# A two-stage Fourier filter and routed experts on one core: which of the first two batches keeps its data on chip between which stages, with one chain of stage 2 for both

## The chip, the core and the metric

The kernel runs on one core of a Trainium2 chip. The metric is the device time of one execution in microseconds (us). A core has four compute engines that run their own instruction queues in order and wait for each other by semaphores: TensorE (PE; its weight loads are listed as PEld), VectorE (DVE), ScalarE (ACT) and GpSimd (POOL). A fifth queue, SyncE (SP), only starts transfers (DMAs). ACT and POOL start transfers too; in the views such starts stand under SPq, ACTq or, for POOL's indirect ones, under POOL itself.

## What is computed

There are 8 batches of 2496 rows with 256 channels. Along the rows each batch is filtered in the frequency domain, and each filtered row then goes through a two-layer network that its token's number selects among 8:

```python
X = np.fft.rfft(x, axis=1)
Y = X * (filt_r + 1j * filt_i)[None]
y = np.fft.irfft(Y, n=2496, axis=1).reshape(8 * 2496, 256)
expert = token_ids * 2654435761 % 8
out[expert == e] = np.maximum(y[expert == e] @ w1[e], 0) @ w2[e]    # for e in 0..7, hidden size 1024
```

All data are float32.

## The kernel before, in words

**The Fourier part** is split into a length of 39 and a length of 64 (39 x 64 = 2496), by matrix products with tables, so each batch has three stages:

- *Stage 1* transforms along 39. Six steps (`u` = 0 to 5) take the batch's rows x, which `load1` brings in three pieces (`v` = 0, 1, 2) of up to 8 x 256 columns.
- *Stage 2* transforms along 64, multiplies by the filter and transforms back along 64. It has ten steps. `forward` (L253) makes two matmuls into pb and four DVE instructions: y = pb x filt (L264), two halves of z (L267), y = y + z (L268). `back` (L271) or `back_c` (L326) makes the matmuls into pc, which ACT copies out. Step u of `stage2` runs forward(u) and then back(u - 1), so that DVE works while PE goes on.
- *Stage 3* transforms back along 39 in six steps (`stage3`, L360): matmuls into pd, a copy into a tile o, the token's own number beside each row (L364), and then one scatter (an indirect DMA of POOL, L377) for each group of rows. It writes each row to its place in the DRAM table xs, where the rows are sorted by expert. A batch has 22 scatters.

Between the stages the axes change places: what lay on partitions must lie along the free axis. There are two ways to do this.

- *Through DRAM*: the stage writes its result to a DRAM tile (d1 after stage 1, d2 after stage 2; ACT starts these writes), and the next one reads it in another layout (`load2`, L245, into t2 tiles; `load4`, L355, into t4 tiles; SP starts these reads). Batches 2 to 7 take this way twice. Stage 1 is then `stage1` (L233) and stage 2's end is `back`.
- *On chip*: stage 1 is written with x as the stationary operand (`stage1_c`, L300), its result `mixed` stays in SBUF, and `turn2` (L316) transposes the columns for two steps of stage 2 on PE, with a copy by ACT. In the same way `back_c` leaves its result `out` in SBUF and `turn4` (L335) transposes it for stage 3. Batches 0 and 1 take this way twice.

**The order.** Nothing is scheduled automatically: a list `todo` (L669 to L694) holds each piece of work with a number, is sorted by it, and is issued in that order. Negative numbers come before the first tile of the expert part, numbers from 0 on are placed in the loop over tiles: `step(i)` issues what has a number below i + 1 between the two layers of tile i. Each engine then works its own queue in that order. Routing has its pieces in the list, too: `count` and `route` (DVE) find each token's expert and place, `later` (POOL, L551) sums corrections, `places` (L558) sends the places to DRAM and back as scatter indices sidx, `experts` finds each tile's expert.

```python
todo += [(-150.4, lambda: first.turn2(0)), (-130.5, lambda: second.turn2(0))]
todo += part2(0, spaced(-150, -130, N_2)) + part2(1, spaced(-130, -105, N_2))
todo += [(t, lambda u=u: second.stage1_c(u)) for u, t in enumerate(spaced(-147.5, -132, NU))]
for bt, at in ((first, spaced(-126, -105, NU)), (second, spaced(-103, -85, NU))):
    todo += [(t - 2.6, lambda bt=bt, u=u: bt.turn4(u)) for u, t in enumerate(at)]
    todo += [(t, lambda bt=bt, u=u: bt.stage3(u)) for u, t in enumerate(at)]
todo += part1(2, spaced(-102, -87, NU), [-128, -127, -126])
```

So batch 0's stage 2 runs first, batch 1's next with batch 0's stage 3 among it, then batch 1's stage 3 with batch 2's stage 1. After that `begin` (L703) starts the fetch of the first tiles' rows.

**The expert part.** Tile i holds 128 rows of one expert from xs. `load` fetches two tiles at once into xg (L729, four DMAs) and their row numbers (L731), `turn` transposes them on DVE into xt (L743), `up` (L753) makes 16 matmuls into ups, which ACT and DVE copy with the maximum against 0 (L757, L759), `down` (L765) makes the second layer, and POOL scatters the result to the output (L769). `weights` (L405, L407) loads an expert's two matrices, 1 MB each, two tiles ahead and only where the expert changes. Tiles 0 to 29 need the rows of batches 0 and 1 alone; a tile's fetch waits for the scatters of its batches. Batches 2 to 7 are worked on inside this loop.

**Buffers that matter.** The tiles `mid` and `wts` are shared by hand: `mixed`, `out`, t1, t2 and g tiles and x of batch 0 are slices of them, and the weights of the first two tiles later take `wts`. The o tiles of batches 0 and 1 have four buffers. The semaphores of transfers go round: the SP and ACT queues have eight together, and a DMA waits for the eighth before it, so no more than eight of theirs are under way; POOL's have eight of their own.

Of the kernel before, what the change touches and what calls it, by code (L numbers as in the profile page):

```python
# [19 lines left out]
P = 128  # L20
# [95 lines left out]
def kernel(  # L116
# [20 lines left out]
    def pool(stack, name, bufs, space=None):  # L137
# [33 lines left out]
             "g": [mid[:, k, :].rearrange("p (s c) -> p s c", c=C) for k in (9, 4)]}  # L171
# [5 lines left out]
    class Batch:  # L177


        def __init__(self, b):  # L180
            self.b = b
            self.d1 = self.d2 = None
            self.x, self.t2, self.t4, self.p = {}, {}, {}, {}
            self.g = None
            if b < 2:

                own = mid[:, 5 * b:5 * b + 5, :].rearrange("p k f -> p (k f)")
                self.mixed = own.rearrange("p (h n s) -> p h n s", h=2, s=NS)
                after = (held[:, 0:NS * C] if b == 0 else mid[:, 0:5, :].rearrange("p k f -> p (k f)"))
                self.out = after.rearrange("p (h n s) -> p h n s", h=2, s=NS)  # L190

        def load1(self, v):
# [9 lines left out]
            for h in range(H):  # L202
                nc.sync.dma_start(out=xt[h:NR:H, 0:n, :],
# [41 lines left out]
        def load2(self, g):  # L245
            t2 = slot("t2")
# [6 lines left out]
        def forward(self, u):  # L253
            ps = fps.tile([P, 2, C], F32, name=f"pb_{self.b}_{u}", tag="f")
            for i in range(2):
                s = 2 * u + i
                rhs = self.t2[u][:, i, :] if self.b < 2 else self.t2[s // SG][:, s % SG, :]
# [13 lines left out]
        def back(self, u):  # L271
# [4 lines left out]
            if u % half == 0:  # L276
                self.g = slot("g")
# [12 lines left out]
        def stage2(self, u):  # L290
            if self.b < 2 and u + 1 < NS // 2:
                self.turn2(u + 1)
            if u < NS // 2:
                self.forward(u)
            if u > 0:
                (self.back_c if self.b < 2 else self.back)(u - 1)
# [3 lines left out]
        def stage1_c(self, u):  # L300
# [4 lines left out]
            for h in range(2):  # L305
                ps = (xps, dps)[h].tile([P, 4, TB], F32, name=f"pa_{self.b}_{u}_{h}", tag="xd"[h])
# [28 lines left out]
        def turn4(self, u):  # L335
# [3 lines left out]
            copy = nc.vector.tensor_copy if self.b else nc.scalar.copy  # L339
            for k in range(0, min(XG, HN + 1 - XG * u), 2):  # L340
# [8 lines left out]
                if rows[0] == rows[1]:  # L349
                    copy(out=self.t4[v][:, j0 + k:j0 + k + 2, :], in_=ps[0:NK])  # L350
                else:
                    for i in range(2):
                        copy(out=self.t4[v][0:rows[i], j0 + k + i, :], in_=ps[0:rows[i], i, :])
# [30 lines left out]
    batches = [Batch(b) for b in range(B)]  # L384

# [28 lines left out]
    for v in range(NV):  # L414
        batches[0].load1(v)
# [4 lines left out]
    nc.scalar.dma_start(out=rt[:], in_=r_dram.ap())  # L420
    nc.vector.tensor_copy(tokno[:], rt[0:NR, G + 2 + NQP:])

    S_PARTS = (slice(0, 4), slice(4, 8), slice(8, 14), slice(14, NS))

    def load_tables(part):
        sl = S_PARTS[part]
# [4 lines left out]
    def load_filter(k, sl):  # L431
        filt = (filt_r, filt_i)[k]
        for q in range(2):
            off, step = (0, C) if q == 0 else (N1 * C, -C)
            nc.sync.dma_start(
# [200 lines left out]

    def part1(b, at, loads=None):
        bt = batches[b]
        if loads is None:
            loads = [at[2 * v] - 2.5 * (at[1] - at[0]) for v in range(NV)]  # L640
# [3 lines left out]
    def part2(b, at, ready=None):  # L644
# [5 lines left out]
        if b < 2:  # L650
# [188 lines left out]
```

## Time and profile before

| What | us |
|---|---|
| three timed runs | 1554.77 (median), 1554.59, 1556.4 |
| the profiled run, and the span of its profile | 1548.5, 1546.7 |
| PE busy, of the span | 1464.9 (95%) |
| DVE, ACT, POOL busy | 532.7 (34%), 234.0 (15%), 378.3 (24%) |
| first matmul of a tile starts | 165.34 |
| one tile in the last third of the loop | 7.03 |

The profile describes one execution. Its page gives busy times of each engine and the span in 40 slices; its views list instructions in order of time. A row of a timeline has start, duration, engine, line of the code, operation, output<-input, the number of instructions that it merges, and in brackets how long the engine stood idle before it and what ended that. The times of such a row are us from the span's start. "issue" in the brackets says that the profile shows nothing that was waited for. A PE row of a float32 product counts two records for each matmul (x8 for four). Shares of busy time over the whole span say little here, as the 165 us before the first tile and the loop after it have different limits; so the stretches are read one by one.

### The profile page before, as it was taken

The page shows a single profiled execution, that of the slowest core. Times are in us where ns is not written, and L with a number is a line of the kernel's source. Part 1 is how long each engine was busy: PE and PEld are TensorE (multiplying, and loading weights), DVE is VectorE, ACT ScalarE, POOL GpSimd, SP SyncE. Part 2 cuts the span into 40 slices and gives each one's busy share as a digit, 9 for nine tenths or more (in the row PEclk, how much of TensorE's full clock was granted, in tenths as well). Part 3 has the DMA queues.
Part 4 walks back from the last instruction along what each step waited for, and adds up shares of the span by engine and source line. Part 5 has one row for each costly group of instructions (what it writes and reads, how often), then busy time and mean ns, then how long its engine had stood idle before and what let it go on. Part 6 is the DMA issues. An engine that isn't in the chain of part 4 may idle for free.

```text
span 1546.7 us, 25542 instructions
## 1 busy us (share of the span) xinstructions
PE 1464.9 (95%) x9340; PEld 1339.3 (87%) x9340; DVE 532.7 (34%) x1004; ACT 234.0 (15%) x401; POOL 378.3 (24%) x384
## 2 busy tenths in 40 slices
PE   7796898989989999999999999999999999999997
PEld 6785687878878999899989999899899999999996
DVE  6772532542244434334333433222212121212121
ACT  4453121112111111101110111000000000000000
POOL 5466102312320133122221323232211111111111
PEclk9998899999999999999999999999999999999999
DMA  8256567548866794684737845552426523132324
GB/s 219 56 182 196 163 198 217 154 131 237 236 197 185 224 277 122 180 226 127 219 90 205 249 117 157 113 160 80 147 75 216 150 55 115 50 96 84 101 84 136
DMA packets 226476, 240.72 MB, mean 156 GB/s; under 512 B 123788, under 2 KB 200127, under 8 KB 219229
## 3 DMA queue, kind: packets, MB, share of 16 engines
q1 hardware_dynamic: 186451, 164.06, 38.6%
q0 software_dynamic: 19120, 43.35, 8.3%
q10 hardware_dynamic: 20778, 31.64, 6.6%
q8 instruction: 76, 1.25, 0.4%
q14 instruction: 51, 0.42, 0.1%
HBM read 415.94 MB, written 75.08 MB: 317 GB/s over the span
## 4 chain that ended last, share of the span: by engine, by line
PE 83%; DMA 6%; issue 5%; DVE 4%; SPq 1%; POOL 0%; ACT 0%; ACTq 0%; DVEq 0%; POOLq 0%
PE ups L753 34%; PE dps L765 33%; PE pb L258 3%; PE pd L220 3%; PE pc L280 3%; PE pa L220 2%; DMA d<-mid 2%; DVE z L267 1%; PE pc L331 1%; DMA wts<-in_x_dram 1%; DMA wts<-in_moe_w_dram 1%; DVE y L268 1%; DMA mid<-d 1%; DVE y L264 1%; PE pa L310 1%
## 5 line engine op out<-in xcount | busy, mean ns | idle before, releaser
L753 PEld LDWEIGHTS ups<-xt,wts 128*128 128x128 f32 x5088 | 594.3, 192 | 14.3 <-issue 3.0
L753 PE MATMUL ups<-xt,wts 128*128 128x128 f32 x5088 | 595.5, 275 | 4.4 <-issue 2.3
L765 PE MATMUL dps<-wts,ht 128*128 128x256 f32 x2544 | 580.1, 381 | 0.6 <-DMA wts<-in_moe_w_dram 0.6
L765 PEld LDWEIGHTS dps<-wts,ht 128*128 128x128 f32 x2544 | 479.8, 191 | 65.8 <-issue 2.4
L769 POOL DMA_INDIRECT out_dram<-osb,no x159 | 156.2, 982 | 883.2 <-DVE osb L768 829.8
L759 DVE TENSOR_SCALAR ht<-ups 128x512 f32<-128x512 f32 x159 | 110.0, 692 | 527.5 <-PE ups L753 512.8
L757 ACT ACTIVATE ht<-ups 128x512 f32<-128x512 f32 x159 | 95.0, 597 | 981.1 <-PE ups L753 741.1
L377 POOL DMA_INDIRECT xs<-o,sidx x176 | 177.0, 1006 | 240.6 <-DVE o L222 148.1
L768 DVE COPY osb<-dps 128x256 f32<-128x256 f32 x159 | 67.5, 425 | 366.2 <-PE dps L765 337.0
L267 DVE TENSOR_TENSOR z<-pb,filt 64x512 f32<-64x512 f32 x160 | 110.2, 689 | 3.5 <-DMA xs<-blank,at_i 1.1
L258 PE MATMUL pb<-mid,d_t 128*128 128x256 f32 x240 | 65.5, 398 | 12.0 <-DMA mid<-d 6.9
L220 PE MATMUL pd<-t,wi_t 120*117 120x256 f32 x320 | 76.0, 380 | 0.4 <-issue 0.4
L264 DVE TENSOR_TENSOR y<-pb,filt 128x512 f32<-128x512 f32 x80 | 54.1, 676 | 62.9 <-PE pb L258 49.0
L280 PE MATMUL pc<-y,e_t 128*128 128x256 f32 x240 | 64.7, 393 | 9.8 <-DVE y L268 8.1
L743 DVE STREAM_TRANSPOSE xt<-xg 128x256 f32<-128x256 f32 x159 | 69.1, 435 | 0.0
L220 PEld LDWEIGHTS pd<-t,wi_t 120*117 120x117 f32 x320 | 55.8, 181 | 10.8 <-issue 1.1
L280 PEld LDWEIGHTS pc<-y,e_t 128*128 128x128 f32 x240 | 45.8, 195 | 20.0 <-issue 6.6
L258 PEld LDWEIGHTS pb<-mid,d_t 128*128 128x128 f32 x240 | 45.0, 199 | 19.3 <-issue 14.0
L283 ACT COPY mid<-pc 128x512 f32<-128x512 f32 x60 | 35.2, 586 | 169.7 <-PE pc L280 163.4
L268 DVE TENSOR_TENSOR y<-y,z 128x512 f32<-128x512 f32 x80 | 59.2, 740 | 2.7
L220 PE MATMUL pa<-x,wf_t 117*120 117x256 f32 x224 | 53.1, 380 | 2.7 <-DMA x<-in_x_dram 1.9
L220 PEld LDWEIGHTS pa<-x,wf_t 117*120 117x120 f32 x224 | 39.6, 183 | 10.0 <-issue 2.7
(117 smaller groups left out, 456.0 us busy)
## 6 DMA issues: line engine op xcount, KB each, us to landing
wts<-in_moe_w_dram SPq DMA_DIRECT2D x322, 1024.0 KB
xg<-xs SPq DMA_DIRECT2D x316, 64.0 KB
mid<-d SPq DMA_DIRECT2D x60, 256.0 KB
d<-mid ACTq DMA_DIRECT2D x60, 256.0 KB
d<-mid ACTq DMA_DIRECT2D x12, 960.0 KB
t<-d SPq DMA_DIRECT2D x12, 960.0 KB
x<-in_x_dram SPq DMA_DIRECT2D x36, 312.0 KB
x<-in_x_dram SPq DMA_DIRECT2D x21, 234.0 KB
```

What stands on the lines that cost most here:

```text
L220: nc.tensor.matmul(out=ps[0:cols * H, k, :], lhsT=w[:], rhs=src[:, 2 * i + k, :], start=True, stop=True)
L258: nc.tensor.matmul(out=ps[:, i, :], lhsT=d_t[:, s, :], rhs=rhs, start=True, stop=True)
L264: nc.vector.tensor_tensor(out=y[:], in0=ps[:], in1=f_t[0][:, sl, :], op=OP.mult)
L267: nc.vector.tensor_tensor(out=z[b], in0=ps[a], in1=f_t[1][a, sl, :], op=OP.mult)
L268: nc.vector.tensor_tensor(out=y[:], in0=y[:], in1=z[:], op=OP.add)
L280: nc.tensor.matmul(out=ps[:, i, :], lhsT=e_t[:, 2 * u + i, :], rhs=pr[:, i, :], start=True, stop=True)
L377: st = nc.gpsimd.indirect_dma_start(out=xs[:], out_offset=bass.IndirectOffsetOnAxis(ap=index, axis=0), in_=rows, in_offset=None, bounds_ch ...
L753: nc.tensor.matmul(out=ps[:, k, :], lhsT=w1[:, dp, fp * P:(fp + 1) * P], rhs=xt[i][:, dp, :], start=(dp == 0), stop=(dp == DP - 1))
L757: nc.scalar.activation(out=dst, in_=ps[:], func=AF.Relu)
L759: nc.vector.tensor_scalar_max(dst, ps[:], 0.0)
L765: nc.tensor.matmul(out=ps[:, 0, :], lhsT=ht[:, fp, :], rhs=w2[:, fp, :], start=(fp == 0), stop=(fp == FP - 1))
L769: st = nc.gpsimd.indirect_dma_start(out=out[:], out_offset=bass.IndirectOffsetOnAxis(ap=xg[i][1].bitcast(I32), axis=0), in_=o[:], in_offse ...
```

## The change

Batch 0 stays on chip from stage 1 to 2 (`stage1_c`, `turn2`) and now goes through DRAM from 2 to 3 (`back`, d2, `load4`). Batch 1 now goes through DRAM from 1 to 2 (`stage1`, d1, `load2`) and stays on chip from 2 to 3 (`back_c`, `turn4`). So batch 1's `turn2` and batch 0's `turn4` are gone. Stage 2 of both is one chain of 20 steps: step k issues turn2 for step k + 1, forward for k and back for k - 1, across the border of the batches. The slices of `mid` and `wts` are given out anew, with slots of their own for batch 1's t2 and batch 0's g tiles. Batch 1's stage 1 takes its accumulators from the pool `fps`.

At the start, a third of batch 0's x loads goes to ACT's queue behind the two small loads of the routing; the loads of filt_r go to POOL's queue, the first two groups each behind a copy of one element that reads batch 0's x; `count` is issued one step of stage 1 later and `places` 0.5 later.

In the list, the first stage 2 steps of batch 2 move from before the first tile into the loop, its `load2` calls move behind the fetch of the first tiles' rows, the first two x pieces of batch 3 are loaded before the loop, and the x loads of batches 4 to 7 get other numbers. The first fetches of xg are split over SP and ACT. The diff, cut to its core:

```diff
+             "g0": [part.rearrange("p (s c) -> p s c", c=C) for part in (mid[:, 9, :], held[:, 4 * SG * C:5 * SG * C])],
+             "t2_1": [held[:, k * SG * C:(k + 1) * SG * C].rearrange("p (s c) -> p s c", c=C) for k in range(4)]}
...
-                nc.sync.dma_start(out=xt[h:NR:H, 0:n, :],
+                (nc.scalar if self.b == 0 and h == 1 else nc.sync).dma_start(out=xt[h:NR:H, 0:n, :],
...
-            t2 = slot("t2")
+            t2 = slot("t2_1" if self.b == 1 else "t2")
...
-            if self.b < 2 and u + 1 < NS // 2:
-                self.turn2(u + 1)
             if u < NS // 2:
                 self.forward(u)
             if u > 0:
-                (self.back_c if self.b < 2 else self.back)(u - 1)
+                self.back(u - 1)
...
     def load_tables(part):
+        if part < 2:
+            nc.gpsimd.tensor_copy(junk[:], first.x[2 * part][0:1, 0, 0:1])
...
-            nc.sync.dma_start(
+            (nc.sync if k else nc.gpsimd).dma_start(
                 out=f_t[k][64 - 64 * k + 32 * q:96 - 64 * k + 32 * q, sl, :],
...
     def part1(b, at, loads=None):
-            loads = [at[2 * v] - 2.5 * (at[1] - at[0]) for v in range(NV)]
+            loads = [max(at[0] - 4, past[3] + .1), max(at[0] - 3, past[5] + .1), at[1] + .1]
+        past[:] = at
...
+    def chain(k):
+        for steps, j in (((Batch.turn2, None), k + 1), ((Batch.forward, Batch.forward), k), ((Batch.back, Batch.back_c), k - 1)):
+            b, u = divmod(j, NS // 2)
+            if 0 <= j < NS and steps[b]:
+                steps[b](batches[b], u)
...
-    todo += [(-150.4, lambda: first.turn2(0)), (-130.5, lambda: second.turn2(0))]
-    todo += part2(0, spaced(-150, -130, N_2)) + part2(1, spaced(-130, -105, N_2))
-    todo += [(t, lambda u=u: second.stage1_c(u)) for u, t in enumerate(spaced(-147.5, -132, NU))]
-    for bt, at in ((first, spaced(-126, -105, NU)), (second, spaced(-103, -85, NU))):
-        todo += [(t - 2.6, lambda bt=bt, u=u: bt.turn4(u)) for u, t in enumerate(at)]
-        todo += [(t, lambda bt=bt, u=u: bt.stage3(u)) for u, t in enumerate(at)]
+    todo += [(-150.4, lambda: first.turn2(0))]
+    todo += [(t, lambda k=k: chain(k)) for k, t in enumerate(spaced(-150, -105, NS + 1))]
+    todo += [(t, lambda u=u: second.stage1(u)) for u, t in enumerate(spaced(-145, -134.4, NU))]
+    todo += [(t, lambda g=g: second.load2(g)) for g, t in enumerate((-132.5, -132.4, -132.3, -132.2, -126))]
+    at = spaced(-123.7, -105, NU)
+    todo += [(t, lambda v=v: first.load4(v)) for v, t in enumerate((-128.4, -128.3, at[1] + .1))]
+    todo += [(t, lambda u=u: first.stage3(u)) for u, t in enumerate(at)]
+    at = spaced(-103, -85, NU)
+    todo += [(t - 2.6, lambda u=u: second.turn4(u)) for u, t in enumerate(at)]
+    todo += [(t, lambda u=u: second.stage3(u)) for u, t in enumerate(at)]
-    todo += part1(2, spaced(-102, -87, NU), [-128, -127, -126])
+    todo += part1(2, spaced(-102, -87, NU), [-130, -129.9, -129.8])
-    todo += part1(3, spaced(2, 7, NU), [.3, 1.5, 3]) + part1(4, spaced(15, 20.5, NU))
+    todo += part1(3, spaced(1, 5.5, NU), [-74.6, -74.5, 1.9]) + part1(4, spaced(15, 20.5, NU))
-    todo += part2(2, [-74, -73] + spaced(.1, 5.5, N_2 - 2), [-78, -77.9, -75, -74.5, .4]) + part2(3, spaced(8.5, 15.5, N_2), 7)
+    todo += part2(2, spaced(.05, 5.5, N_2), [-75, -74.9, -74.8, -74.7, .6]) + part2(3, spaced(8.5, 15.5, N_2), 7)
...
-        lds = [nc.sync.dma_start(out=g[32 * q:32 * q + 32, 0:4 * n, :],
+        lds = [(nc.scalar if i < 2 and q % 2 else nc.sync).dma_start(out=g[32 * q:32 * q + 32, 0:4 * n, :],
```

## The prediction, made before the changed kernel was run

> **What bounds the kernel now.** I read the page's 40 slices first, then the busy time of each engine by stretch, then the timelines of the queues between 60 and 170 us. TensorE bounds the loop over tiles; the head, before the first tile, is bounded by something else.
>
> ```profile
> core 0: us, PE busy (x) PEld busy (x) DVE busy (x) ACT busy (x) POOL busy (x), PEclk, DMA share, GB/s
> 0.00:165.30 165.30, 125.50 (x756) 108.71 (x756) 96.42 (x184) 71.96 (x123) 90.13 (x93) 0.91 0.60 171
> 165.30:460.00 294.70, 272.33 (x1591) 241.90 (x1592) 111.59 (x199) 45.51 (x79) 68.20 (x68) 0.97 0.65 190
> 460.00:1530.00 1070.00, 1061.31 (x6962) 983.73 (x6961) 322.19 (x615) 115.93 (x198) 218.63 (x222) 1.00 0.50 143
> ```
>
> Each row is a stretch, with busy us and, in brackets, instructions of each engine. From 460 us on PE is busy for 1061.3 of 1070 us: nothing in the change reaches that. The head (first tile at 165.3) has 39.8 us without a matmul, and 165 to 460 has 22.4. So what can be won or lost lies in those two.
>
> GpSimd's timeline shows what sets the head's end. It has the scatters of batches 0 and 1 into xs, 44 of them:
>
> ```profile
> 69.35 2.09 POOL L566 DMA_DIRECT2D sidx<-slots  x3 [1.63 <-DMA slots<-eid_i]
> ...
> 82.00 1.08 POOL L377 DMA_INDIRECT xs<-o,sidx  x1 [10.56 <-ACT wts L324]
> 83.39 1.03 POOL L377 DMA_INDIRECT xs<-o,sidx  x1 [0.30 <-issue]
> ...
> 115.11 0.90 POOL L377 DMA_INDIRECT xs<-o,sidx  x1 [0.30 <-issue]
> 118.19 0.99 POOL L377 DMA_INDIRECT xs<-o,sidx  x1 [2.17 <-ACT o L222]
> ...
> 148.26 0.99 POOL L377 DMA_INDIRECT xs<-o,sidx  x1 [2.08 <-ACT o L217]
> 149.78 0.90 POOL L377 DMA_INDIRECT xs<-o,sidx  x1 [0.53 <-ACT o L217]
> ```
>
> A scatter takes 0.99 us and the next starts 0.30 later, 1.30 us each, so 44 take 57.2. From 82.0 to 150.7 are 68.7: 11.5 us are gaps, for which the brackets name the releaser. PE, DVE and SP around it:
>
> ```profile
> 69.50 2.07 PE L331 MATMUL pc<-e_t,y 128*128 128x128 f32 x8 [4.25 <-DVE y L268]
> ...
> 78.19 1.89 PE L220 MATMUL pd<-t,wi_t 120*117 120x256 f32 x8
> ...
> 155.99 3.75 PE L258 MATMUL pb<-mid,d_t 128*128 128x256 f32 x8 [6.90 <-DMA mid<-d]
> 160.95 2.07 PE L280 MATMUL pc<-y,e_t 128*128 128x256 f32 x4 [1.21 <-issue]
> 165.34 5.28 PE L753 MATMUL ups<-xt,wts 128*128 128x128 f32 x32 [2.32 <-issue]
> ...
> 266.40 2.05 PE L258 MATMUL pb<-mid,d_t 128*128 128x256 f32 x4 [5.09 <-issue]
> ```
>
> ```profile
> 162.76 1.39 DVE L267 TENSOR_TENSOR z<-pb,filt 64x512 f32<-64x512 f32 x2 [1.15 <-DMA xs<-blank,at_i]
> ...
> 164.80 0.44 DVE L743 STREAM_TRANSPOSE xt<-xg 128x256 f32<-128x256 f32 x1
> ```
>
> ```profile
> 72.33 2.39 SPq L203 DMA_DIRECT2D wts<-in_x_dram  x3
> ...
> 151.55 2.44 SPq L249 DMA_DIRECT2D mid<-d  x4
> 154.37 1.92 SPq L729 DMA_DIRECT2D xg<-xs  x4
> ```
>
> After the last scatter the first tile's rows (xg, L729) are not fetched at once: SP first issues four loads of batch 2's stage 2 (L249, 2.44 us). PE and DVE then do two steps of that stage, the transpose of the rows (164.80) stands on DVE behind them, and the step before it waits 1.15 us on the blank rows' scatter. So 14.6 us pass between the last scatter's end and the first matmul of a tile.
>
> **The Trainium skill.** "DMA: Bandwidth & Descriptors", Issuing engines are not separate DMA queues: all queues end on the same 16 engines, and a second issuing engine saves only issue time. The trace agrees for the head: DMA share is 1.00, 0.97 and 0.94 from 10 to 40 us at 213 to 238 GB/s, so moving head loads to ACT and GpSimd buys about 1 us. "GPSIMD Engine Reference", Key points: GpSimd shares its SBUF interfaces with DVE instructions of two SBUF inputs. The trace agrees: the add y (L268) takes 2.51 us instead of 0.69 where it meets GpSimd's L556 at 38.9. "TensorE: Matmul & The Clock Gate", Part 1: after an idle window the clock is halved. The trace agrees: x32 ups takes 5.28 us at 165.3 and 3.73 later.
>
> **The change, part by part.** Instruction order and semaphore waits come from the two built programs.
>
> 1. Work removed: batch 1's turn2 (10 x 0.64 us on PE, 10 x 0.59 on ACT) and batch 0's turn4 (5.5 x 0.87 on PE, some 11 x 0.54 on ACT), 11.2 us of PE and 12 of ACT. Batch 1's stage 1 (1.73 for 1.78 us) and batch 0's back (0.87 for 0.89) stay alike. I book nothing for it directly: GpSimd's queue hides it. It counts through the next steps.
>
> 2. Batch 0's stage 2 is paced by DVE: y_0 starts at 24.34, y_9 ends at 69.44, with 2.79 us a step. Head loads reordered: 1 us at most, and x of batch 1 (v=1) now waits for the first d2 write, so I book 0. GpSimd's `later` starts some 3 us later (it first issues 8 filter loads behind two one-element copies that wait for x of batch 0, and `count` comes one group later); of its three sums that held y back by 0.4, 1.8 and 1.5 us, two should miss. I take 3 us (bounds -1 and 4): y_9 ends at 66.4, the last back matmul at 67.4.
>
> 3. Batch 0's pass through DRAM, the added wait, in a row: ACT copies and issues the last d2 writes by 69.2 (0.6 + 2 x 0.55); they land at 71.7 (d<-mid took 2.35 us where idle, 12.24 at its worst). In the program SP's fifth load of batch 2's x waits for just that write (no more than eight hardware DMAs of SP and ACT are open), and five such loads stand ahead of load4: 5 x 0.80 = 4.0. Then t4's 960 KB plus what is left of x, about 1.25 MB at the 265 GB/s seen from 73 to 84 us: 4.7; to land, 1.3 (2.35 for 256 KB, less 1.0 at that rate). t4 at 81.7. Queued behind pd_0 on PE is all of batch 1's forward from u=3 on; it stalls with it. ACT's d1 and d2 writes share the eight open places with SP's loads, and the copies of pt and pc stand behind them on ACT: up to 4 us, within step 2's bounds, since DVE has y to do meanwhile.
>
> 4. pd_0 at 81.7, against 78.19. PE has idled, so its first half takes 1.7, ACT's copy 0.6, start of the scatter 0.7: first scatter at 84.7, 2.7 us later (bounds 80 and 92, the latter with t4 landing 7 us later). In the kernel before, that first scatter waited 1.9 us for DVE's L364; now that write is early.
>
> 5. Scatters: 57.2 us stay. Gaps: 11.5 now. Batch 1's forward no longer holds turn2 or waits for batch 0's tail, so its t4 is ready about 3 us before GpSimd asks (by my chain pc_9 at 110, GpSimd at 115), and the 2.2 us at 118.19 go. I take 5 us (bounds 2 and 11). Last scatter ends at 84.7 + 57.2 + 5 = 146.9, against 150.7.
>
> 6. Entry to the loop: the load2s of batch 2 now stand behind xg, its stage 2 steps are inside the loop, and xg's loads are split over SP and ACT. Landing of the last scatter 1.8, issue 1.0, landing of xg 2.7, transpose 0.44, start 0.4: 6.3 us. First tile at 153.2 against 165.3: **-12.1**.
>
> 7. Paid back in the loop: pb_0, pb_1 and pc_0 of batch 2, 3 x 0.87 = **+2.6**, and pc_0's wait for y_0 in tile 0, **+1.9** (2.79 less 0.87).
>
> 8. Batch 3's stage 1 ends one and a half tiles earlier and its first six loads come before the loop. The 1.9 us wait for x at 208.6 goes: **-1.9**. So should the 5.1 us before 266.4, where load2 of batch 3 hung on a d1 write that landed in 12.24 us, and 2.3 us of half clock after it (2.05 for 1.03, 4.89 for 3.62): **-7.4** (bounds -7.4 and 0).
>
> 9. Against it: 14 loads (2.1 MB and 1.9 MB) now stand between xg and the weights of tile 2 on SP. No row shows what that costs; bounds 0 and 6 (the rest of those 4 MB at 190 GB/s, 21 us, over the two tiles of some 12 us that hide them, and one slow landing). I take **+3**. The later batches' x loads moved by under two tiles: booked at 0, the PE waits for x there are nil now.
>
> Sum: -12.1 + 2.6 + 1.9 - 1.9 - 7.4 + 3 = -13.9 us on a span of 1546.7. The timed runs (1554.59 to 1556.4) lie some 8 us above that span; I subtract from their median: 1554.8 - 13.9 = 1540.9, say **1541**.
>
> **The rivals.** *A later t4* (chance 0.22): x of batch 2 and load2 of batch 1 slow the pass, first scatter at 91, batch 1's work bunches behind it. For: five loads ahead of load4 on one queue. Against: 73 to 84 us shows 265 GB/s. It gives 6.5 us less: 1547. *GpSimd without gaps, loop without new waits* (0.13): gaps 2 and step 9 at nil: 1535, or less with an earlier chain. *DRAM passes at their worst* (0.08, slower): every landing takes the 12.24 us the trace shows at 243.7. Batch 1's d1 write then lands 7.7 late (I allow it 4.5) and holds pc_9 on PE, d2's write 9.7 late, t4's read 6.2 late: first scatter at 108.3, all else equal +23.6, so 1564. It decides from a first scatter at 98.6 on (84.7 + 13.9). For: the trace has such a landing. Against: that was amid weights of 1 MB, and 50 to 70 us has almost no traffic (1 and 10 GB/s).
> *It cancels* (0.06): half of that delay, or no gain in the loop and a late t4: 1555. That the edit does not move the work is excluded: the built order shows it.
>
> **How the numbers follow.** The forecast has 0.51. 0.2% (3.1 us) is about what a measurement of this kernel can tell from no change. Faster by more: 0.51 + 0.22 + 0.13 = 0.86; within: 0.06; slower: 0.08. The range runs from 1533 (forecast with gaps 2, step 9 nil and an early chain) to 1553 (A later t4 with step 8 at nil, nearly), leaving out the worst passes, half of the cancelling case and the end of the fast one.
>
> **What would show it.** First L377 scatter at 80 to 92, the last of the 44 ended by 150; first ups about 6 us after that and near 153, with no matmul of stage 2 between; the stall before pb of batch 3 gone; PE waits of tiles 0 to 4 within 3 us of now. Wrong if the first scatter comes after 98, if gaps on GpSimd stay at 11, or if tile 2 waits for weights.

## The result, and the profile after

| | before | after |
|---|---|---|
| median of the timed runs, us | 1555.59 | 1580.59 |
| all of them | 1554.59 to 1557.04 | 1576.14, 1576.5, 1584.68, 1584.76 |
| ratio after / before, 95% interval | | 1.016 (1.012 to 1.0199) |
| span of the profile | 1546.7 | 1582.9 |
| y_9 of batch 0 ends | 69.44 | 75.24 |
| first and last scatter of batches 0 and 1: start, end | 82.00, 150.68 | 103.03, 175.81 |
| first tile: start of its first matmul | 165.34 | 181.33 |
| the loop: from there to the end of the span | 1381.4 | 1401.6 |

The change makes the kernel 1.6% slower, where 0.9% faster was forecast. The last two rows split the loss of 36 us between the two profiles: 16 ahead of the first tile and 20 after it. The profiled executions are not the median ones: before's (1548.5) is 7.1 us below its median, the changed kernel's (1584.68) 4.1 above, so the profiles differ by 36 us and the medians by 25. The busy time of each engine by stretch, cut at the new start of the first tile and again 294.7 us later, says the same:

```profile
core 0: us, PE busy (x) PEld busy (x) DVE busy (x) ACT busy (x) POOL busy (x), PEclk, DMA share, GB/s
0.00:181.30 181.30, 118.55 (x576) 96.72 (x577) 93.52 (x176) 58.85 (x100) 90.86 (x101) 0.84 0.70 198
181.30:476.00 294.70, 272.21 (x1601) 242.46 (x1602) 117.20 (x207) 45.96 (x80) 70.95 (x71) 0.98 0.68 200
476.00:1566.00 1090.00, 1066.87 (x6956) 987.27 (x6955) 322.54 (x616) 115.86 (x198) 217.49 (x221) 0.99 0.48 140
```

From 181 to 476 PE is idle for 22.5 us, as it was before (22.4). From 476 us on it is idle for 23.1 us of 1090, where it had been idle for 8.7 of 1070: something was lost there, where the forecast saw nothing to lose. GpSimd's timeline shows the head:

```profile
103.03 1.10 POOL L377 DMA_INDIRECT xs<-o,sidx  x1 [24.10 <-ACT o L225]
...
134.90 0.98 POOL L377 DMA_INDIRECT xs<-o,sidx  x1 [2.97 <-ACT o L220]
...
143.43 0.99 POOL L377 DMA_INDIRECT xs<-o,sidx  x1 [6.11 <-ACT o L225]
...
174.91 0.90 POOL L377 DMA_INDIRECT xs<-o,sidx  x1 [0.53 <-ACT o L220]
```

The first scatter comes 18.3 us later than forecast, and two gaps of 2.97 and 6.11 us that end on ACT stand among the 44. What the first scatter waited for is seen in the timeline of SP's queue in the changed kernel:

```profile
66.98 7.71 SPq L252 DMA_DIRECT2D wts<-d  x8
75.53 2.45 SPq L206 DMA_DIRECT2D wts<-in_x_dram  x3
78.08 11.26 SPq L206 DMA_DIRECT2D x<-in_x_dram  x6
89.45 1.07 SPq L358 DMA_DIRECT2D t<-d  x2
```

ACT's timeline in the same profile, with its own issues of d2 (ACTq):

```profile
47.33 5.20 ACTq L290 DMA_DIRECT2D d<-wts  x2
52.57 1.07 ACT L225 COPY mid<-pa 120x512 f32<-120x512 f32 x2 [5.27 <-DMA d<-mid]
...
78.58 1.26 ACTq L290 DMA_DIRECT2D d<-mid  x2
86.05 1.25 ACT L334 COPY mid<-pc 128x512 f32<-128x512 f32 x2 [7.51 <-DMA d<-mid]
```

And PE's, with what ended the idle time before each row in brackets:

```profile
53.21 2.59 PE L223 MATMUL pa<-x,wf_t 117*120 117x256 f32 x8 [2.60 <-ACT mid L225]
...
100.07 3.73 PE L223 MATMUL pd<-t,wi_t 120*117 120x256 f32 x8 [15.94 <-DMA t<-d]
```

The last d2 writes of batch 0 (ACT, L290) are issued by 79.84, but by the trace's records of landings they land only at 85.35 and 85.95. The place that the first of them holds among the eight open transfers is the one that the second of SP's six x loads (L206) waits for; it starts at 85.37, after 6.5 us. So the six take 11.26 us until the last is issued, and only then t<-d (L358) goes out at 89.45. PE stands for 15.94 us until it has landed. Earlier, ACT stands in one pair of d2 writes, issued from 47.33 on: the second of them starts at 52.07. It waits for the place of batch 1's first d1 write (960 KB), which was issued at 42.73 and lands at 52.05. PE waits 2.6 us for ACT at 53.21.

In the loop, these are the long waits of PE's timeline from 420 us on:

```profile
432.23 5.38 PE L784 MATMUL dps<-wts,ht 128*128 128x256 f32 x16 [3.82 <-DMA wts<-in_moe_w_dram]
...
580.14 5.36 PE L784 MATMUL dps<-wts,ht 128*128 128x256 f32 x16 [4.90 <-DMA wts<-in_moe_w_dram]
...
711.71 2.04 PE L261 MATMUL pb<-mid,d_t 128*128 128x256 f32 x4 [9.15 <-DMA mid<-d]
```

In the kernel before, no wait for weights or for mid<-d of over 1.5 us stands there. The three waits are 17.9 us, and the instructions after each run at half clock for a while (dps takes 5.36 in place of 3.62).

### The profile page after: what moved, and what is told of

Read it like the earlier page. It is cut to its first block, busy times and chain, and to the rows that moved or that the text cites. A ratio compares the mean times of both kernels' runs of the same rounds, so it can differ in the third digit from the quotient of the medians.

```text
span 1582.9 us, 25239 instructions
## 1 busy us (share of the span) xinstructions
PE 1464.2 (93%) x9172; PEld 1332.3 (84%) x9172; DVE 535.8 (34%) x1004; ACT 221.3 (14%) x379; POOL 381.2 (24%) x394
## 4 chain that ended last, share of the span: by engine, by line
PE 71%; issue 13%; DMA 6%; POOL 4%; DVE 3%; SPq 1%; ACT 1%; another core or an unknown queue 0%; POOLq 0%; ACTq 0%; DVEq 0%
PE ups L772 29%; PE dps L784 29%; PE pd L223 3%; PE pb L261 3%; POOL xs L377 2%; PE pc L283 2%; PE pa L223 2%; DMA wts<-in_moe_w_dram 2%; DMA t<-d 1%; POOL out_dram L788 1%; DMA d<-mid 1%; DVE z L270 1%; DMA out_dram<-osb,no 1%; PE pa L311 1%; SPq L206 1%
## 5 line engine op out<-in xcount | busy, mean ns | idle before, releaser
L772 PEld LDWEIGHTS ups<-xt,wts 128*128 128x128 f32 x5088 | 594.2, 192 | 18.9 <-issue 10.6
L223 PE MATMUL pd<-t,wi_t 120*117 120x256 f32 x320 | 80.5, 396 | 15.9 <-DMA t<-d 15.9
L283 PE MATMUL pc<-y,e_t 128*128 128x256 f32 x280 | 76.8, 399 | 17.1 <-DVE y L271 16.7
L283 PEld LDWEIGHTS pc<-y,e_t 128*128 128x128 f32 x280 | 53.7, 197 | 29.3 <-issue 10.5
L223 PE MATMUL pa<-x,wf_t 117*120 117x256 f32 x248 | 59.5, 383 | 3.3 <-ACT mid L225 2.6
L286 ACT COPY mid<-pc 128x512 f32<-128x512 f32 x66 | 38.6, 585 | 170.7 <-PE pc L283 155.3
L223 PEld LDWEIGHTS pa<-x,wf_t 117*120 117x120 f32 x248 | 44.1, 184 | 11.4 <-ACT mid L225 3.0
```

The costliest lines, as they stand in the source:

```text
L223: nc.tensor.matmul(out=ps[0:cols * H, k, :], lhsT=w[:], rhs=src[:, 2 * i + k, :], start=True, stop=True)
L283: nc.tensor.matmul(out=ps[:, i, :], lhsT=e_t[:, 2 * u + i, :], rhs=pr[:, i, :], start=True, stop=True)
L772: nc.tensor.matmul(out=ps[:, k, :], lhsT=w1[:, dp, fp * P:(fp + 1) * P], rhs=xt[i][:, dp, :], start=(dp == 0), stop=(dp == DP - 1))
```

## The experiments

The table has all runs beside the changed kernel's first. Chips differ (the kernel before had medians of 1545.8, 1559.1, 1546.4 and 1546.5 us beside these runs), so times are compared by their ratio to it on the same chip. The other columns come from one profile each. A star marks profiles with a stand of several engines that is told of below; in the changed kernel's two profiles it delays the first tile by an estimated 3 to 12 us.

| Run | ratio to before (95%) | first scatter | first tile | loop |
|---|---|---|---|---|
| changed kernel again* | 1.0129 (1.0106 to 1.0153) | 101.1 | 173.9 | 1399.9 |
| t4_first | 1.0099 (1.0066 to 1.0132) | 89.8 | 158.0 | 1397.9 |
| old_x | 1.0035 (1.0022 to 1.0048) | 101.9 | 169.4 | 1375.6 |
| t4_first_old_x | 0.9972 (0.9958 to 0.9986) | 92.5 | 159.8 | 1379.8 |
| entry_only | 0.9956 (0.9937 to 0.9975) | 81.7 | 155.1 | 1380.0 |
| entry_again | 0.9938 (0.9914 to 0.9962) | 81.9 | 154.7 | 1379.8 |
| pass1_only* | 0.9976 (0.9961 to 0.9991) | 88.7 | 170.3 | 1388.0 |
| pass0_only* | 0.998 (0.9962 to 0.9997) | 87.1 | 162.3 | 1382.5 |
| old_head* | 0.9981 (0.9962 to 1.0001) | 101.5 | 180.8 | 1380.4 |
| d2_sp | 0.9973 (0.9955 to 0.9991) | 94.5 | 163.7 | 1378.5 |
| x6v2 | 1.0131 (1.0091 to 1.017) | 102.3 | 169.5 | 1399.1 |
| x6v1 | 1.0121 (1.0083 to 1.016) | 102.1 | 169.3 | 1397.4 |
| x7v1 | 1.0092 (1.0062 to 1.0122) | 102.5 | 169.4 | 1396.3 |
| x7v01 | 1.0091 (1.0057 to 1.0125) | 101.1 | 169.8 | 1387.6 |
| x45_old | 1.0164 (1.013 to 1.0197) | 102.7 | 171.2 | 1397.8 |

### The late t4: its place on SP

```diff
-    todo += part1(2, spaced(-102, -87, NU), [-130, -129.9, -129.8])
+    todo += part1(2, spaced(-102, -87, NU), [-128.2, -128.1, -128.0])
```

> The changed kernel, but SP issues load4 of batch 0 (t<-d, v=0 and 1) ahead of the nine loads of batch 2's x, not behind them. Theory A (t4 is late because it stands behind x loads that wait for open places of DMA): the last d2 writes are issued at about 79.8 us as now, t<-d is issued at about 84 in place of 89.5, pd_0 starts at 90 to 94 in place of 100.1, the first scatter at 93 to 97 in place of 103.0, and the first tile starts 6 to 10 us earlier than 181.3; median about 1572. Theory B (the late steps of batch 0's stage 2 and the DRAM pass itself make t4 late, the x loads only share the bandwidth): the first scatter stays at 100 or later and the median lies within 4 us of the changed kernel's 1580.6.

Theory A holds, by more than it gave (first scatter at 89.8 in place of 93 to 97). The timeline of SP's queue in this run has t<-d ahead of the x loads:

```profile
79.05 0.95 SPq L358 DMA_DIRECT2D t<-d  x2
80.10 3.15 SPq L206 DMA_DIRECT2D wts<-in_x_dram  x3
83.35 10.13 SPq L206 DMA_DIRECT2D x<-in_x_dram  x6
```

ACT's timeline has the last d2 writes of batch 0, and its next copy, which waits for them to land:

```profile
75.72 1.11 ACTq L290 DMA_DIRECT2D d<-mid  x2
79.08 0.69 ACT L334 COPY mid<-pc 128x512 f32<-128x512 f32 x1 [3.39 <-DMA d<-mid]
```

PE's has the start of pd_0:

```profile
86.86 3.74 PE L223 MATMUL pd<-t,wi_t 120*117 120x256 f32 x8 [4.89 <-DMA t<-d]
```

The writes are issued by 76.83 and have landed 2.2 us later. Then t<-d goes out at 79.05, before the x loads, and PE has its data 7.8 us after that. So the pass itself costs 10.0 us from the last write's issue to pd_0. In the changed kernel the same took 20.2 us (79.84 to 100.07). The difference of 10.2 us has three parts. With x loads ahead of them the writes hold up SP for 5.5 us in place of 2.2; the x loads that are left take 4.1 us until t<-d is issued; and the read takes 10.6 us in place of 7.8. So the x loads do more than stand ahead of t<-d: they also make the writes slow that it has to wait for. In old_x, with the same order, these took 7.2 us to land, in t4_first_old_x 3.1.

### The loop: the x loads of batches 4 to 7

```diff
-            loads = [max(at[0] - 4, past[3] + .1), max(at[0] - 3, past[5] + .1), at[1] + .1]
+            loads = [at[2 * v] - 2.5 * (at[1] - at[0]) for v in range(NV)]
```

> The changed kernel, but the x loads of batches 4 to 7 get the due times that they have in the kernel before; the head and the entry to the loop are untouched. Theory A (the loop's loss comes from these loads, which now stand ahead of loads of stage 2 and of weights): the first tile stays at 181 us, the PE waits mid<-d of 9.1 us near 710 and wts of 4.9 us near 580 go, and the median falls by 12 to 16 us to about 1566. Theory B (the loop's loss comes from batches 2 and 3, whose stages were moved, or from landings that fall differently whenever anything is moved): waits of the same sum, about 20 us, turn up at other places and the median lies within 4 us of 1580.6.

The loop takes 1375.6 us in place of 1399.9 to 1401.6, with the head unchanged: theory A, and somewhat more than it gave. The profile is of this kernel's fastest run; by the ratios the gain is 15 to 19 us. Both edits together:

> Both edits together: load4 of batch 0 ahead of batch 2's x, and the due times of the kernel before for the x loads of batches 4 to 7. If both theories A hold and the two losses are apart in time, the gains add: about 1580.6 - 9 - 14 = 1557, within 4 us of the kernel before. If either theory B holds, 1565 or more.

The gains add. Against this run, t4 behind x costs 0.63% (1.0035 less 0.9972, 9.8 us of 1555.6), the moved x loads 1.27% (1.0099 less 0.9972, 19.8 us).

Which loads they are, four single-batch edits and one for batches 4 and 5 should tell:

```diff
x6v2, x6v1:
-    ... part1(6, spaced(36, 46, NU))
+    ... part1(6, spaced(36, 46, NU), [32, 33, 38.1])          # x6v1: [32, 35.2, 37.77]
x7v1, x7v01:
-    ... part1(7, spaced(50, 60, NU))
+    ... part1(7, spaced(50, 60, NU), [46, 49.2, 51.77])       # x7v01: [45.8, 49.2, 51.77]
x45_old:
+    ... part1(4, ..., [12.7, 14.5, 16.4]) ... part1(5, ..., [18.5, 20.5, 22.5])
```

> The changed kernel with one number altered: the last three x loads of batch 6 (v=2) are due at 38.1 in place of 37.77, that is one tile later, behind the weights and rows that SP loads for the tile in between. They take the buffer that stage 1 (u=1) of the same batch frees on PE; at 37.77 SP reaches them one tile before PE has got there. Theory A (SP stands about 13 us in this load and the weights behind it come late): the issue of these three loads falls from 13 us to about 2.5, the dps wait for wts of 4.9 us near 580 goes, with 1.7 us of half clock behind it, and the loop from the first tile on takes 1393 to 1396 us in place of 1400 to 1402; about -6.5 us on the whole. Theory B (the weights are late because of the bandwidth): the wait stays or moves, the loop takes 1399 or more.

A miss: SP still stands 13.57 us at 542.8, and the wait is 5.9 us. The load that stands is another one, of v=1.

> The changed kernel with one number altered: the three x loads of batch 7 (v=1) are due at 49.2 in place of 47, that is behind the first six loads of stage 2 of batch 6 and not ahead of them. Theory A (three x loads ahead of these loads on SP make the first pb of batch 6 wait): the pb wait for mid<-d of 9.1 us near 710 falls to at most 2 us, with 2.5 us of half clock behind it, and the loop from the first tile on takes 1389 to 1393 us in place of 1400 to 1402; about -10 us on the whole. Theory B (the pb wait comes from late writes of d1 of batch 6, which the x loads do not touch): it stays at 6 us or more.

Half a miss: the wait falls from 9.1 to 5.0 us, not to 2.

> The changed kernel with one number altered: the three x loads of batch 6 (v=1) are due at 35.2 (as in the kernel before) in place of 33. In the built order the third of them waits for the place that a d2 write of batch 5 holds; in three traces SP stands 13.1 to 13.6 us there, and the second weights of that tile come behind. Theory A (that stand makes the dps wait near 580): no stand of SP over 6 us near 545 to 560, the dps wait of 4 to 6 us near 570 goes with 1.7 us of half clock, and the loop from the first tile takes 1392 to 1395 us in place of 1400 to 1402. Theory B (the write lands late in any case and SP stands at another load, with the same cost): loop 1399 or more.

Between the theories. SP stands all the same, now 11.4 us in mid<-d and not in x, but the wait for weights falls to 2.4 us, and the loop to 1397.4. SP's queue in the changed kernel's timeline shows the stand and what is behind it:

```profile
556.64 13.07 SPq L206 DMA_DIRECT2D x<-in_x_dram  x3
569.76 1.18 SPq L252 DMA_DIRECT2D mid<-d  x2
571.49 0.21 SPq L408 DMA_DIRECT2D wts<-in_moe_w_dram  x1
```

ACT's timeline there has the writes of d2 of batch 5:

```profile
558.38 1.10 ACTq L290 DMA_DIRECT2D d<-mid  x2
```

The second and third of the three x loads wait for the places that these two d2 writes of batch 5 hold. The first write is issued from 558.38 on and lands at 567.23, 8.9 us later; the second x load starts at 567.25. The weights (571.49) are behind them. A write of d2 is slow at this place in the kernel before, too: it took 7.1 us (542.30 to 549.42), and SP stood with it in two loads of mid<-d (9.35 us from 540.57 on). There the weights behind it came in time.

> The changed kernel with the x loads of batch 7, v=0 and v=1, at their old due times: 45.8 and 49.2 in place of 46 and 47. With v=1 alone moved back the pb wait near 710 fell from 9.1 to 5.0 us only; v=0 still stood one tile later than before, among tiles of 7 us, where SP was 4 us behind PE. Theory A (both together hold the six loads of stage 2 of batch 6 back): the pb wait is gone (under 1 us), and the loop takes 1387 to 1391 us in place of 1400 to 1402. Theory B (another cause, such as the waits before it): 3 us or more stay, loop 1394 or more.

Theory A: the wait is gone. SP's queue in the changed kernel's timeline, from the first x loads of batch 7 (L206) to the loads of stage 2 of batch 6 (L252):

```profile
689.21 2.46 SPq L206 DMA_DIRECT2D x<-in_x_dram  x3
691.71 0.55 SPq L358 DMA_DIRECT2D t<-d  x1
692.61 0.09 SPq L408 DMA_DIRECT2D wts<-in_moe_w_dram  x1
692.81 3.74 SPq L748 DMA_DIRECT2D xg<-xs  x4
696.66 2.19 SPq L750 DMA_DIRECT2D no<-xs  x1
700.60 0.38 SPq L406 DMA_DIRECT2D wts<-in_moe_w_dram  x1
703.24 2.45 SPq L206 DMA_DIRECT2D x<-in_x_dram  x3
705.73 3.72 SPq L252 DMA_DIRECT2D mid<-d  x6
```

The same stretch of SP's queue in this run:

```profile
669.84 2.46 SPq L206 DMA_DIRECT2D x<-in_x_dram  x3
...
679.96 1.78 SPq L748 DMA_DIRECT2D xg<-xs  x4
...
683.99 0.09 SPq L406 DMA_DIRECT2D wts<-in_moe_w_dram  x1
685.70 3.70 SPq L252 DMA_DIRECT2D mid<-d  x6
```

PE's timeline of this run has the first pb of batch 6, with no wait before it:

```profile
690.16 1.03 PE L261 MATMUL pb<-mid,d_t 128*128 128x256 f32 x4
```

These tiles are 7 us long. In the first excerpt three more x loads (v=1) stand right ahead of L252, which starts at 705.73, though PE was ready for the data at 702.56 (711.71 less the wait of 9.15). In the second no x load stands there, the loads of v=0 are one tile earlier, and L252 starts at 685.70, 4.5 us before pb. The four loads of xg took 3.74 us to issue in the first and 1.78 in the second; why is open.

> The changed kernel with the x loads of batches 4 and 5 at their old due times, those of 6 and 7 as changed. Theory A (each batch's loads cost at their own place): the dps wait of 3.8 to 5.1 us near 420 to 432 goes with 1.7 us of half clock, those of 4 to 6 us near 570 and of 9 us near 705 stay, and the loop takes 1393 to 1396 us. Theory B (what the first of these loads delay sets the later waits off): the later waits go too, loop 1385 or less; or nothing goes, 1399 or more.

The wait near 420 (at 432 in the changed kernel's first profile) goes and the later two stay (4.0 and 9.0 us): each has its own place. The loop falls by 2 to 4 us only. Against 1400.7 (mean of two profiles) the parts are 3 for batches 4 and 5, 3 for v=1 of batch 6, and 13 for batch 7: 19 in all, where all of them together gave 18 (t4_first to t4_first_old_x) to 25 (old_x). These parts are from one profile each. By ratio x6v2, x6v1 and x45_old (1.0121 to 1.0164) are not told apart from the changed kernel (1.016 and 1.0129), and the two edits of batch 7 (1.0092 and 1.0091) hardly.

### The entry alone

On the kernel before, only these lines are changed; its head, its ways through DRAM and its x loads of batches 4 to 7 stay.

```diff
-    todo += part1(3, spaced(2, 7, NU), [.3, 1.5, 3]) + ...
+    todo += part1(3, spaced(1, 5.5, NU), [-74.6, -74.5, 1.9]) + ...
-    todo += part2(2, [-74, -73] + spaced(.1, 5.5, N_2 - 2), [-78, -77.9, -75, -74.5, .4]) + ...
+    todo += part2(2, spaced(.05, 5.5, N_2), [-75, -74.9, -74.8, -74.7, .6]) + ...
-        lds = [nc.sync.dma_start(out=g[32 * q:32 * q + 32, 0:4 * n, :],
+        lds = [(nc.scalar if i < 2 and q % 2 else nc.sync).dma_start(out=g[32 * q:32 * q + 32, 0:4 * n, :],
```

> The kernel before with only the entry to the loop changed: batch 2's stage 2 and its loads behind the first rows' loads, batch 2's stage 2 wholly inside the loop, the first rows' loads split over SP and ACT, batch 3's stage 1 and x loads earlier. The head up to the last scatter is that of before. Theory A (my steps 6 to 9): first tile 8 us earlier (157 in place of 165.3), paid back 2.6 + 1.9 in the loop, the 5.1 us stall of batch 3's pb and the 1.9 us wait for x gone: median 1542 to 1550. Theory B (the time won at the entry is paid back wholly in the loop): within 3 us of 1555.6.

> The kernel before with only the entry to the loop changed, once more, for a second profile and a comparison on the same chip as the runs beside it. Its ratio to the kernel before was 0.9956 (0.9937 to 0.9975); I expect 0.993 to 0.998, the first tile 8 to 10 us before that of the kernel before in an execution of the same kind, and a loop from there of 1378 to 1382 us.

Theory A, twice: 0.44% and 0.62% faster than before, the fastest of all versions run here. GpSimd's timeline in entry_only has the last scatter:

```profile
147.67 0.89 POOL L377 DMA_INDIRECT xs<-o,sidx  x1 [0.30 <-issue]
```

PE's has the first tile:

```profile
155.13 5.47 PE L753 MATMUL ups<-xt,wts 128*128 128x128 f32 x32 [10.25 <-DVE xt L743]
```

From the scatter's end (148.56) to the first tile are 6.6 us, 14.7 before. The loop takes 1.5 us less than before, so on balance nothing is paid back.

### The passes and the head's loads

In the next three, the entry of the change and the old x loads are kept. Each pass is undone by itself, with the slices of mid and wts that this needs, and then the order of the head's loads.

```diff
pass1_only: batch 0 stays on chip; head's loads as before; batch 2's x as in the change
-  ((Batch.back, Batch.back_c), k - 1)
+  ((Batch.back_c, Batch.back_c), k - 1)
-    todo += [(t, lambda v=v: first.load4(v)) for v, t in ...]
+    todo += [(t - 2.6, lambda u=u: first.turn4(u)) for u, t in enumerate(at)]
pass0_only: batch 1 stays on chip; t<-d first; head's loads as before
-  ((Batch.turn2, None), k + 1)
+  ((Batch.turn2, Batch.turn2), k + 1)
-    ... second.stage1(u)) for u, t in enumerate(spaced(-145, -134.4, NU))]
+    ... second.stage1_c(u)) for u, t in enumerate(spaced(-147.5, -132, NU))]
old_head: t4_first_old_x with the head's loads as before
```

> One part alone: only batch 1 passes through DRAM (from stage 1 to 2, d1), batch 0 stays on chip throughout as in the kernel before (its stage 3 begins with turn4 on PE and ACT); head loads as before, entry to the loop as in the change, old due times of the x loads. Theory A (batch 0's pass is what makes the first scatter late; batch 1's pass only takes work off PE and ACT): first scatter at 80 to 84 as before, gaps among the scatters 4 to 8 us, last scatter ended by 146, first tile at 151 to 154, median 1533 to 1538 beside 1539 of the entry alone. Theory B (batch 1's d1 comes late, its forward holds PE): first scatter as before, but gaps of 12 us or more, 1543 or more.

> The other part alone: only batch 0 passes through DRAM (from stage 2 to 3, d2), batch 1 stays on chip throughout as in the kernel before (turn2 on PE and ACT); head loads as before, t<-d ahead of batch 2's x, entry as in the change, old due times of the x loads. Theory A (batch 0's pass makes the first scatter late by the write and the read of DRAM, some 6 to 9 us): first scatter at 88 to 92, gaps 5 to 10, first tile at 158 to 162, median 1541 to 1548. Theory B (the pass is hidden behind other work): first scatter at 84 or earlier, median 1539 or less.

> The changed kernel with both mendings (t<-d ahead of batch 2's x, old due times of the x loads of batches 4 to 7), and in addition the head's loads as in the kernel before: x of batch 0 and both filters on SP, no loads on GpSimd, count and places at their old times. Theory A (the reordered head loads cost time, since they start GpSimd's sums later and put SP's x loads of batch 1 and ACT's writes of d1 and d2 behind each other): y_9 of batch 0 ends 2 to 6 us earlier than in the run with both mendings, the first scatter at 87 to 90 in place of 92.5, median about 1537 where that run had 1541. Theory B (the order of the head's loads matters little, the bandwidth is used up in both): first scatter within 2 us of 92.5, median within 2 us of 1541.

By time none of the three is told apart from t4_first_old_x (0.9972). All lie above the entry alone, though their intervals overlap with one or both of its own (0.9937 to 0.9975, 0.9914 to 0.9962). For pass0_only theory A is the nearer one (first scatter 87.1, ratio 0.998). pass1_only fits neither: its first scatter is at 88.7, though batch 0 reads nothing back from DRAM. SP's timeline of the run shows the first x loads of batch 2, which go into wts:

```profile
70.15 2.44 SPq L207 DMA_DIRECT2D wts<-in_x_dram  x3
```

ACT's has the last copy of batch 0's stage 2, whose result lies in wts too in this kernel:

```profile
80.36 0.69 ACT L335 COPY wts<-pc 128x512 f32<-128x512 f32 x1 [10.23 <-DMA wts<-in_x_dram]
```

The change puts these x loads at -130, ahead of that last step (about -128.6 in the list); in the kernel before they stand behind it. The product was ready at 73.0, and ACT waited for the x loads to land. So some 7 us of this late first scatter come from the place of x and not from batch 1's pass, and the run does not price that pass by itself. Its gaps (19 us) can't be read for the stand in its profile.

The end of y_9 of batch 0 tells something of the passes: 69.3 us in entry_only, 71.0 and 71.1 with one pass, 75.2 with both (one profile each). With both and the old head's loads it is 84.0: in that profile ACT waits 7.53 us for filt_i at 64.13. That execution is 6.8 us above the median of its kernel, so how much of it belongs to the program is open. Theory A for old_head finds no support, neither in y_9 nor in the ratio; by time the order of the head's loads made no difference that these runs tell.

```diff
-                    nc.scalar.dma_start(out=self.d2[:, a0:a0 + SG, :],
+                    (nc.scalar if self.b else nc.sync).dma_start(out=self.d2[:, a0:a0 + SG, :],
```

> The changed kernel with both mendings (t<-d first, old due times of x), and the writes d2 of batch 0 issued by SP in place of ACT. In the changed kernel ACT stands 4.9 to 5.2 us in one pair of these writes at 47 us, since no place of the eight open transfers is free, and PSUM is not emptied meanwhile (PE waits 2.6 us at 53). Theory A (this standing of ACT makes y_9 late): ACT's stand is gone, y_9 of batch 0 ends 3 to 5 us earlier than 75 us and the first scatter comes at 86 to 89. Theory B (the places themselves are short, whoever issues): SP stands instead, its x loads of batch 1 come later, and the first scatter is at 92 or later.

Theory B. SP stands now, and PE waits all the same, for an ACT copy that waited 8.04 us for an earlier write of d2 to land. SP's queue in the timeline of d2_sp:

```profile
38.95 10.52 SPq L442 DMA_DIRECT2D filt<-in_filt_i_dram  x2
49.59 4.06 SPq L290 DMA_DIRECT2D d<-mid  x2
```

PE's timeline of the same run:

```profile
57.92 2.07 PE L261 MATMUL pb<-wts,d_t 128*128 128x256 f32 x4 [5.15 <-ACT mid L286]
```

y_9 ends at 76.9, no earlier than with ACT as the issuer (75.2). What holds the place is the same in both: batch 1's first d1 write, here issued at 40.87 and landed at 49.13. SP's second load of filt_i starts at 49.14, and the d2 writes come behind it.

### The changed kernel once more

> The changed kernel, unaltered, once more, with a second profile. The first profile of it has one stall of ACT, DVE and SP together between 126 and 134 us (ACT waited 5.17 us for something the trace calls remote), and its runs lie on two levels 8 us apart. If that stall is an accident of single executions, the first tile starts near 170 us here, as in the run with the old x loads (same head, 169.4), the gaps among the 44 scatters are about 5 us in place of 16, and the ratio to the kernel before is 1.010 to 1.016. If it belongs to the kernel, it is there again at the same place and the first tile is at 178 or later.

In between: the first tile is at 173.9, the ratio as expected. Eight profiles have this very head. In the six whose edits are in the loop alone, the first tile is at 169.3 to 171.2, and the gaps among the 44 scatters are 3.1 to 4.8 us (last end less first start less 57.2). In the changed kernel's own two profiles they are 15.6 and 10.3, and ACT stands. Its timeline in the first:

```profile
133.67 0.69 ACT L334 COPY mid<-pc 128x512 f32<-128x512 f32 x1 [5.17 <-remote]
134.23 0.37 ACT L220 COPY o<-pd 117x256 f32<-117x256 f32 x1
```

Here ACT waited 5.17 us for something "remote", and DVE and SP stand at the same time. In the second profile it is 6.2 us before 140.7. So an estimated 10 to 12 us of the first profile's late first tile, and 3 to 5 of the second's, belong to the execution and not to the program; the first scatter (101 to 103) isn't touched. The profile of the kernel before has such stands too (ACT 2.3, DVE 7.4 us near 143), so the gaps of 11.5 us that step 5 set out from hold some of it: the entry alone, with the same head and no stand, has 9.7 and 8.2. Six profiles have stands, the two of the first table and the four taken beside a kernel before of 1559.1 us; the other eleven, where the kernel before had 1545.8 to 1546.5 us, have none. So they go with the chip or the time of the run. What is waited for is open.

## Why the prediction was wrong

Two costs were set too low, the entry to the loop gained much as forecast, and the passes themselves gained nothing. By ratios: entry -0.44 to -0.62%, passes and head's loads in a good order about +0.25 (0.9972 against the mean of entry, 0.9947), t4 behind x +0.63, x loads of batches 4 to 7 +1.27: together +1.6%, where 1.6 and 1.3 were measured. The +0.25 is hardly clear of nothing; the forecast had the last scatter 3.8 us earlier (146.9 for 150.7), which is -0.25%.

**Step 9 failed most**, in its last clause, "The later batches' x loads moved by under two tiles: booked at 0, the PE waits for x there are nil now". The reason looked at who waits for x, but the loads cost by what is behind them on SP: weights, rows, and L252. One or two tiles decide there: x7v01 moves two of batch 7's loads back by one and two tiles, and the wait of 9.15 us is gone. (One of them, v=1, had in fact moved by 2.2 tiles, from 49.2 to 47.) The term measured 15 to 20 us (old_x against the changed kernel, t4_first_old_x against t4_first). The +3 for tile 2's weights, on the other hand, was nothing: no wait stands there.

**Step 3 was mis-sized**: t4 at 81.7, in fact 100.1. Three terms carry the 18.4 us. The last d2 write ends its issue at 79.8, not 69.2: 10.6 us, of which 8.8 are y_9's (step 2). From there to t<-d it takes 9.6 us, not 6.5 (2.5 + 4.0): the place was there only when the write itself had landed, after 5.5 us, and the five loads behind it took 4.1, as forecast. The read takes 10.6, not 6.0. With t<-d first the last two are 2.2 and 7.8, so the order on SP costs 10.2 us.

**Step 2 was wrong in sign.** It let y_9 end 3 us earlier (66.4), and the bound of 4 us later was too narrow: 75.2, 5.8 later. "ACT's d1 and d2 writes share the eight open places ... up to 4 us, within step 2's bounds, since DVE has y to do meanwhile" (step 3) named the mechanism; DVE did not have y to do, as PSUM, where PE's products lie, was not emptied and PE waited (53.21). In DVE's timeline y_5 ends at 52.6, as before (52.4), and y_6 at 61.5 in place of 55.3: the whole delay arises there. d2_sp shows that the places, not ACT, are short, and the d1 write that holds one lands 9.3 us after its issue, where the prediction had allowed 4.5. The 3 us that step 2 hoped for failed by themselves: GpSimd's sums still held y_1 and y_3 by 2.2 and 1.7 us, 3.9 in place of 3.7.

Step 4 follows from 3: from pd_0 to the first scatter 2.96 us, 3.0 forecast. **Step 5 was right in its number**: gaps of 3.1 to 4.8 us in executions without the stand, 5 forecast; the entry alone, with the head of before, has 8.2 and 9.7. Whether its mechanism is right isn't shown: every such head starts its scatters 5 to 18 us later than forecast, which gives batch 1's work that much more time, so part of it may be luck. **Step 6 was right**: 5.3 to 7.6 us from the last scatter to the first tile in all profiles with the new entry, 6.3 forecast. **Steps 7 and 8** were near: pc_0 waits 2.05 us (1.9), the wait for x is gone, the pb wait of batch 3 fell from 5.1 to 1.7 and not to nil. The entry alone makes the loop 1.4 to 1.6 us shorter, where steps 7 to 9 together gave 1.8. Step 1's removed work could buy nothing here: PE stood 15.9 us for t4. It wasn't tried by itself.

The rival *A later t4* named the cause in the head, and its 91 us lies between the 89.8 and 92.5 of the two runs with t<-d first. *DRAM passes at their worst* had the sign: the first scatter came at 101 to 103, past its 98.6. Of its mechanism a part is there. The last d2 writes took some 6 us to land, not 12.24, but batch 1's d1 write took 9.3 us in the head, and it cost through the place that it held, not through the data that were waited for. A slow d2 write stands in the loop as well (8.9 us at 558), where it was not looked for. None of the rivals had the x loads of the later batches.

## What to carry to other kernels

A load that is moved is priced by what it is moved ahead of on its queue, and by the open places that it takes, not by who waits for its own data. Where a few transfers may be open, one slow write stops every later load of the queue, so a load with time to spare stays behind those with none. Parts of an edit that were made together are worth trying alone: the entry to the loop gained 0.5% by itself, and no run with a pass through DRAM was faster than it.

## What was unexpected

A d2 write of 256 KB landed 2.2 us after its issue in the head with t<-d first, about 6 us after it with x loads of batch 2 ahead of it, and 8.9 us after it in the loop at 558, among loads of weights of 1 MB. Who issues a transfer made no difference here: with SP in place of ACT the stand moved (10.5 us on SP) and y_9 stayed. And in six of seventeen profiles, all from where the kernel before ran slower too, ACT, DVE and SP stand together, in the changed kernel for 4 to 7 us, for something that the trace only calls remote; the first tile of the same head was at 169.3 to 181.3 us.
